# Fused attention and gated-MLP block on one core: where a kept tail of x stands, when the words of A11 are made, which queue stores the last round, and the order of the last sums

## The chip, the cores and the metric

The kernel runs on 1 core of one Trainium2 chip. The metric is device time in microseconds of one execution. The engines are TensorE (PE, its weight loads PEld), VectorE (DVE), ScalarE (ACT), GpSimd (POOL) and SyncE (SP); GpSimd and SyncE also issue the DMAs.

## The reference

```python
# x: 2048 x 576, wqkv: 576 x 1728, wo: 576 x 576, w_gate, w_up: 576 x 4608, w_down: 4608 x 576, all float32
xn = _layernorm(x, axis=-1)
s = _A_ref(xn, A_wqkv, A_wo)     # linear attention, 32 heads: phi(q) (phi(k)^T v) / (phi(q) . sum phi(k)), then @ wo
g = _silu(_B_ref(xn, B_w_gate, B_w_up, B_w_down))   # h = gelu(xn @ w_gate) * (xn @ w_up); h @ w_down
return x + s * g
```

## The kernel before

**Float32 from words.** A float32 operand is kept as two words: `hi`, a rounded copy that ScalarE writes, and `lo`, the rest, which VectorE subtracts (`cut_w`, `cut_two`, `cut`, `make_words`). A product is three matmuls: hi.hi, hi.lo, lo.hi.

**Three stages.** Up to about 210 us the attention's q, k and v are made, from 210 to 277 us the attention's output `s`; then come the gate and up projections (277 to 1073 us), then the down projection (to the end).

**Gate and up.** The two projections are 36 matrices, `q` = 0 to 35: even ones gate, odd ones up, 256 columns each. Rows and columns are halved, and each matrix is done with 7 block products instead of 8, on sums of blocks: weight blocks A11, S2, S1, S3, A12, S4, A22 against x blocks B11, T2, T1, T3, B21, B22, T4. x stands in two blocks of 1024 positions, s = 0 and s = 1, both halves of a product for both blocks at once. The products write into PSUM tiles named `al` (first and fifth), `be` (second), `ga` (third and sixth), `de` (fourth and seventh): the fifth to seventh accumulate onto what the first, third and fourth left there, so VectorE must have read it before.

288 input columns per half don't divide by 128: the last 32, the tail, are multiplied by themselves. The tail's words of x stand in plane 2 of one of the T tiles, and `TAIL` names which T tile of which block carries which of the two column halves. A tail's matmuls are the last of a product's early half and of its late half. The tail of the first column half (c = 0) is used by the fifth and the seventh product, that of the other by the third and the sixth.

Each product is worked in two halves, an early one and a late one. In step n the program issues the early half of product n, then what stands behind product n - 2 (`post_0` to `post_6`: reading PSUM, gelu or the multiplication with the up value, and the work of `todo`), then the late half of product n - 1. ScalarE and VectorE take their instructions in that order, so what is put in `todo[0]` stands in VectorE's queue in front of the sums of `post_1` and `post_2`. `todo` holds the preparation of the next matrix (`mat_pieces`: words of A11, of the sums S1 to S3, of A12 and A22, of S4), the sums of its blocks on GpSimd (`mat_sums`), the load of the one after it, and events.

Block 0 of x doesn't fit beside the attention's data. Its tiles are stored to HBM when they are made (`keep`, `form_apart`; 90 to 130 us) and loaded back (`back`) shortly before 277 us: B11, T2, T1 and T3 by GpSimd's queue, then B21, matrix 1, B22 and T4, in this order, by SyncE's. Their places in SBUF are those of attention data, which come free with the last matmul of `s`.

**h and its sums.** The 18 gate and up pairs form 9 macros (`m` = 0 to 8) of 4 matrices. The down projection also uses fewer products: 26 products `p` on sums of blocks of h. Those sums are added by GpSimd while the matrices run (`ADDS`, `add_up`), at hooks counted 7 to a matrix and 28 to a macro, and every value in `FORM` is stored to HBM (`put_out`). The sums of macro m run into the first matrices of macro m + 1. In the last macro, m = 8, the order is `ADDS_LAST`, the stores go by GpSimd's queue, and what is left behind the last matrix is added by VectorE.

**Down.** For each p and k tile, h is loaded in 5 units (`load_unit`), cut into words (`cut`, unit number u = 5p + k), and multiplied by words of w_down (`make_words`, in two parts: the first five k tiles and the last four). `down_first` gives the hooks of the last matrix the first loads, words and cuts; `down_all` does the rest, with `cut(u + 2)` ahead of the matmuls of unit u.

Of the kernel before, what the change touches and what calls it, by code (L numbers as in the profile page):

```python
# [8 lines left out]
F32 = mybir.dt.float32  # L9
# [47 lines left out]
NM = NG // 2  # L57
# [35 lines left out]

MAIN = ((0, 0), (0, 2), (2, 0), (1, 1), (1, 3), (3, 1))
XW = (0, 1, 3, 4)
TAIL = ({"T4": 0, "T1": 1}, {"T4": 0, "T3": 1})
TR = P // 2

X_SLOT = {"B11": 0, "B21": 1, "B22": 3, "T1": 9, "T3": 10, "T2": 11, "T4": 2}
# [3 lines left out]
def block_kernel(ctx, tc, x, xe, xt, wq_d, wkv_d, wo, wgu_d, wd_d, out):  # L103
    nc = tc.nc
# [52 lines left out]
    def dma(out, in_, eng=None):  # L157
        tc.keep_in_program_order((eng or nc.sync).dma_start(out=out, in_=in_))
# [21 lines left out]
    xo, xf, xstat, store = [{}, {}], [{}, {}], {}, {}  # L180
# [167 lines left out]
    def kept_words(nm, o):  # L348

        if nm in TAIL[0]:  # L350
            return o.rearrange("p k t -> p (k t)")
# [4 lines left out]
    def kept_place(nm, d):  # L356

        if nm in TAIL[0]:
            return d.rearrange("p k t -> p (k t)")
        return d.rearrange("p (a b) t -> p a (b t)", a=2)  # L360

    def kept(s, nm):
        store[s, nm] = d = dr.tile(
            [P, 5 if nm in TAIL[0] else 4, TBN], F32, name=f"kept_{s}_{nm}"
        )
        return d

    def keep(s, nm, o):
        if (s, nm) in store:
            for k in (0, 3):  # L370
                dma(out=store[s, nm][:, k : k + 2], in_=o[:, k : k + 2].bitcast(F32))
            return
        d = kept(s, nm)
        dma(out=kept_place(nm, d), in_=kept_words(nm, o.bitcast(F32)))

    def tail(s, b, o):

        h = s * TR
        for j in range(2):
            v = xf[s][BS[b][j]][:, 2, :]  # L380
            r, low = (slice(i + j * KR, i + (j + 1) * KR) for i in (h, TR - h))
            act(o[r], v[r], AF.Copy)
            vec("tensor_sub", o[low], v[r], o[r].bitcast(F32))
# [4 lines left out]
    def form_lo(s, nm, o):  # L388
        vec("tensor_sub", o[:, 3:5], xf[s][nm][:, 0:2], o[:, 0:2].bitcast(F32))
        if nm in TAIL[s] and nm != "T4":  # L390
            tail(s, TAIL[s][nm], o[:, 2, :])

# [189 lines left out]
    def run(todo, n=None):  # L582
        for _ in range(len(todo) if n is None else min(n, len(todo))):
            todo.pop(0)()
# [71 lines left out]
    at = {}  # L656
# [240 lines left out]
    raw, sums, wt = {}, {}, {}  # L897
# [34 lines left out]
    def quarters(q):  # L932
        return raw[q][:, 0:4].rearrange("p (j k) (f c) -> p j f k c", j=2, f=2)

    def cut_w(o, src):

        act(o[:, :, 0:2, :], src, AF.Copy)
        vec("tensor_sub", o[:, :, 2:4, :], src, o[:, :, 0:2, :].bitcast(F32))
# [14 lines left out]
    def mat_pieces(q):  # L953

        if q >= NQ:
            return [[] for _ in range(7)]

        def raws_(q=q):
            rv = quarters(q)
            if q % 2 == 0:  # L960
                cut_w(wt["b"][:, 1:3], rv[:, 1])
            else:
                cut_w(wt["b"][:, 1:2], rv[:, 1, 0:1])
                cut_w(wt["b"][:, 0:1], rv[:, 1, 1:2])
            cut_tail(q)

        return [
            [lambda: cut_w(wt["a"][:, 0:1], quarters(q)[:, 0, 0:1])],
            [], [],
            [lambda: cut_w(wt["a"][:, 1:4], sums["sm"][:, 0:3])],  # L970
            [raws_],
            [
                lambda: cut_w(wt["b"][:, 3:4], sums["sm"][:, 3:4]),
                lambda: cut_two(wt["last"], sums["last"]),
            ],
            [],
        ]
# [115 lines left out]
    HOOKS = 28  # L1093
# [30 lines left out]
            free[place_of[m, v]] = at  # L1124

    def put_out(m, v, at):
        eng = nc.gpsimd if m == NM - 1 else nc.sync
        dma(out=hs_d[m][:, FORM.index(v)], in_=value(m, v), eng=eng)
        used(m, v, at + 1)

# [80 lines left out]
    def load_reg(at, nm, third=None):  # L1211
        if at not in reg:
            b = big(REG[at], [P, ODD_W if REG[at] in ODD else REG_W], F32, f"b_{at}")
            reg[at] = b[:, 0 : KT * HALF].rearrange("p (k d) -> p k d", k=KT)
        j, c = int(nm[0]) - 1, int(nm[1]) - 1
        par, f = divmod(KP[j], 2)
        src = wd_d[par::2, :, f, c * HALF : (c + 1) * HALF].rearrange("g p d -> p g d")
        k = slice(0, KT) if third is None else slice(3 * third, 3 * third + 3)
        dma(out=reg[at][:, k], in_=src[:, k])
# [42 lines left out]
    def cut(u):  # L1262
        p, k = divmod(u, NU)
        if p >= NP:
            return
        hi, lo = hi_place(p, k), raw_v[p, k]
        hi_v[p, k] = hi
        src = lo.bitcast(F32)
        act(hi, src, AF.Copy)
        vec("tensor_sub", lo, src, hi.bitcast(F32))  # L1270
# [54 lines left out]
    def make_words(p, c):  # L1325

        if p >= NP or p in SHARED or (p, c) in made:
            return
        made.add((p, c))
        hi, lo = (w[c] for w in word_tiles(p))  # L1330
        src = reg[FROM[p]][:, HALVES[c]]
        if PROD[p][2]:
            act(hi, src, AF.Copy, scale=-1.0)
            vec(
                "scalar_tensor_tensor", lo, src, -1.0, hi.bitcast(F32),
                op0=ALU.mult, op1=ALU.subtract,
            )
        else:
            act(hi, src, AF.Copy)
            vec("tensor_sub", lo, src, hi.bitcast(F32))  # L1340
# [101 lines left out]
    def down_first():  # L1442

        return [
            [lambda: load_reg("22", "22")],
            [lambda: load_reg("42", "42")],
            [],
            [lambda: load_unit(0, 0), lambda: load_unit(0, 1), lambda: make_words(0, 0)],
            [
                lambda: load_unit(0, 2), lambda: load_unit(0, 3), lambda: load_unit(0, 4),  # L1450
                lambda: make_words(0, 1), lambda: cut(0),
            ],
            [lambda: load_reg("32", "32"), lambda: cut(1)],
            [],
        ]

# [5 lines left out]
    def down_all():  # L1462
        late = []
        last = NP - 1
        for u in range(NP * NU):
            p, k = divmod(u, NU)
            n = KT * p + 2 * k
            for at in sorted(events):
                if at <= H_END + n // 2:
                    run_events(at)  # L1470
            if p in LOADS and k < 3:
                load_reg(*LOADS[p], k)
            if k == 0:
                for o, e in ENDS.items():
                    if e == p:
                        load_sx(o)
            if k < 2:
                change(p + 1, k)
                if p in SHARED:
                    make_words(p + 1, k)  # L1480
            elif k < 4:
                make_words(p + 1, k - 2)
                if p + 1 in SHARED and p:
                    make_words(p + 2, k - 2)
            if p == last and k == 0:
                read(p - 1)
                late += closings(p - 1)
            if p == last and k == 1:
                run(late, 1)
            cut(u + 2)  # L1490
            if p == last and k == 2:
                break
            for kt in range(*UNITS[k]):
                down_mm(p, kt, range(TT))
            load_unit(p + 1, k)
            run(stores)
            if p == last:
                continue
            if k == 1 and p:
                read(p - 1)  # L1500
                late += closings(p - 1)
            else:
                run(late, 2)
        run(late)
        run(stores)
        o = next(o for o, e in ENDS.items() if e == last)
        for j in (TT - 2, TT - 1):
            add_in(o, j, last)
        for j in range(TT):
            for kt in range(UNITS[2][0], KT):  # L1510
                down_mm(last, kt, (j,))
            late += close_last(o, j, last, j >= TT - 2)
            run(late, len(late) - 1)
        run(late)
# [166 lines left out]
    def form_apart(nm):  # L1681

        f = xf[0][nm]
        d = kept(0, nm)
        hi, lo, last = (slot([P, 2, TBN], F32R, f"xo_0_{nm}_{i}") for i in range(3))
        act(hi, f[:, 0:2], AF.Copy)
        vec("tensor_sub", lo, f[:, 0:2], hi.bitcast(F32))
        tail(0, TAIL[0]["T4"], last[:, 0])
        dma(out=d[:, 0:2], in_=hi.bitcast(F32))
        dma(out=d[:, 2:4], in_=lo.bitcast(F32))  # L1690
        dma(out=kept(0, "T4")[:, 2], in_=last[:, 0].bitcast(F32))

    behind = {
        (0, 0): [
# [54 lines left out]
    def first_matrix():  # L1749
        w_tile("a", 15)  # L1750
        return mat_pieces(0)
# [17 lines left out]
        (0, 1): [lambda: scale(1, 0, 1), lambda: halve(1, 0, 1)],  # L1769
        (0, 2): [lambda: scale(1, 2, 3, 4), lambda: halve(1, 2, 3, 4)],  # L1770
        (0, 3): [lambda: back("T1"), lambda: mat_sums(0)],
        (1, 0): [lambda: pieces.extend(first_matrix()), lambda: run(pieces[0])],
        (1, 1): [lambda: run(pieces[3])],
    }
    pieces = []
    for tb in (2, 3, 0, 1):
# [85 lines left out]
```

## Time and profile before

| | |
|---|---|
| runs | 1452.13, 1450.04, 1450.32 us; median 1450.32 |
| profiled execution | 1454.09 us, span 1452.4 us, mean granted TensorE clock 0.996 |
| TensorE busy | 1435.6 us (99%) |
| VectorE, ScalarE, GpSimd busy | 1006.7, 578.2, 542.7 us |
| DMA | 228.16 MB, 157 GB/s over the span |

In timelines a row is: start, duration, engine, line, operation, output<-inputs with buffer numbers left out, and in brackets the idle time before it with what ended it. xo is block 1 of x, xr the reloaded block 0; `_B` and `_T` are the B and T blocks. wa and wb hold weight words; wa the A11 and the sums S1 to S3, wb the others. spot_h, spot_m and spot_g are places of h and its sums, hs their store in HBM; raw is the loaded weight matrix, raw_a, raw_b and raw_h loaded units of h, bd the down projection's PSUM. Matmul rows are half-width tiles in pairs, one for each block. eps_t rows are marks by which ScalarE follows TensorE.

### The profile page before, as it was taken

How to read it: one execution, taken by the hardware profiler on the slowest of the kernel's cores; microseconds unless marked ns; L12 is line 12 of the kernel's file. 1: busy time of each engine (PE TensorE's matmuls, PEld its weight loads, DVE VectorE, ACT ScalarE, POOL GpSimd, SP SyncE). 2: the span in 40 equal slices, each digit the busy share in tenths (PEclk: the TensorE clock that was granted, in tenths of full speed). 3: DMA queues.
4: the chain of work that ended last, by engine and by line, in shares of the span. 5: the costliest groups of instructions: out<-in, count | busy, mean ns of one | idle time of the engine just before them, and what ended most of it. 6: DMA issues, size and time to landing. Idle time of an engine off the chain costs nothing.

```text
span 1452.4 us, 29230 instructions
## 1 busy us (share of the span) xinstructions
PE 1435.6 (99%) x11656; PEld 1361.9 (94%) x11656; DVE 1006.7 (69%) x1519; ACT 578.2 (40%) x1249; POOL 542.7 (37%) x556
## 2 busy tenths in 40 slices
PE   9999999989999999999999999999999999999998
PEld 8989989889999999999999999999889999999998
DVE  7788666245666656657555666656768978989897
ACT  6354365333222333322333222333236555545454
POOL 3342340115755557475465755557532000000000
PEclk9999999999999999999999999999999999999999
DMA  5444115512332314233232322314279888767886
GB/s 213 172 192 155 45 36 189 215 46 74 132 113 103 132 55 160 95 120 114 78 141 74 136 109 102 132 55 160 77 268 359 259 263 254 244 191 233 280 290 218
DMA packets 120579, 228.16 MB, mean 157 GB/s; under 512 B 11674, under 2 KB 45370, under 8 KB 119802
## 3 DMA queue, kind: packets, MB, share of 16 engines
q1 hardware_dynamic: 117258, 214.82, 43.6%
q0 software_dynamic: 3040, 11.27, 2.1%
q8 instruction: 92, 1.51, 0.4%
q14 instruction: 45, 0.37, 0.1%
q10 hardware_dynamic: 144, 0.20, 0.0%
HBM read 144.93 MB, written 81.27 MB: 156 GB/s over the span
## 4 chain that ended last, share of the span: by engine, by line
PE 89%; DVE 5%; DMA 2%; issue 1%; ACT 1%; SPq 0%; POOL 0%; ACTq 0%; DVEq 0%; POOLq 0%
PE bd L152 21%; PE ga L152 17%; PE de L152 15%; PE al L152 15%; PE kv L152 7%; PE be L152 6%; PE s L152 4%; PE q L152 2%; DMA raw_h<-hs 1%; DMA xr_T<-kept_T 1%; PE kv_a L152 1%; DVE raw_h L149 1%; DVE xo_T L149 1%; DVE wa L149 0%; DVE sx L149 0%
## 5 line engine op out<-in xcount | busy, mean ns | idle before, releaser
L155 POOL TENSOR_TENSOR sums<-raw 128x256 f32<-128x256 f32 (+1 forms) x108 | 70.4, 652 | 165.0 <-DMA raw<-in_wgu_dram 124.0
L152 PE MATMUL de<-xr_T,wa 64*128 64x512 f32 x486 | 128.8, 389 | 0.0
L152 PE MATMUL de<-xo_T,wa 64*128 64x512 f32 x486 | 128.6, 389 | 0.0
L152 PE MATMUL kv<-wkv,xo_B 128*128 128x412 f32 (+2 forms) x662 | 125.0, 347 | 0.1
L152 PEld LDWEIGHTS kv<-wkv,xo_B 128*128 128x128 f32 x662 | 120.2, 188 | 1.5 <-ACT xo_B L146 0.6
L152 PE MATMUL de<-xo_T,wb 64*128 64x512 f32 x486 | 121.6, 386 | 0.0
L152 PE MATMUL ga<-xo_T,wa 64*128 64x512 f32 x486 | 121.6, 386 | 0.0
L152 PE MATMUL de<-xr_T,wb 64*128 64x512 f32 x486 | 121.6, 386 | 0.0
L152 PE MATMUL ga<-xr_T,wa 64*128 64x512 f32 x486 | 121.6, 386 | 0.0
L149 DVE TENSOR_TENSOR wa<-raw,wa 128x256 fp32r<-128x256 f32 x54 | 48.4, 897 | 102.0 <-ACT wa L146 102.0
L152 PE MATMUL bd<-w_head,hi 128*128 128x288 f32 x516 | 117.7, 294 | 0.0
L152 PE MATMUL ga<-xo_B,wb 64*128 64x512 f32 x432 | 112.2, 393 | 2.2 <-DVE spot_m L149 2.2
L152 PE MATMUL ga<-xr_B,wb 64*128 64x512 f32 x432 | 112.0, 393 | 0.0
L152 PE MATMUL al<-xr_B,wb 64*128 64x512 f32 x432 | 109.9, 387 | 0.0
L152 PE MATMUL al<-xr_B,wa 64*128 64x512 f32 x432 | 109.5, 386 | 0.0
L152 PE MATMUL al<-xo_B,wa 64*128 64x512 f32 x432 | 109.5, 386 | 0.0
L152 PE MATMUL al<-xo_B,wb 64*128 64x512 f32 x432 | 109.5, 386 | 0.0
L152 PE MATMUL be<-xo_T,wa 64*128 64x512 f32 x432 | 109.4, 386 | 0.0
L152 PE MATMUL be<-xr_T,wa 64*128 64x512 f32 x432 | 109.4, 386 | 0.0
L146 ACT ACTIVATE hi<-raw_h 128x1024 fp32r<-128x1024 f32 x59 | 62.4, 1059 | 86.1 <-PE bd L152 58.0
L152 PEld LDWEIGHTS de<-xo_T,wa 64*128 64x128 f32 x486 | 90.3, 186 | 4.0
L152 PEld LDWEIGHTS de<-xr_T,wa 64*128 64x128 f32 x486 | 90.1, 186 | 3.1
(300 smaller groups left out, 4754.4 us busy)
## 6 DMA issues: line engine op xcount, KB each, us to landing
raw_h<-hs SPq DMA_DIRECT2D x176, 256.0 KB
raw<-in_wgu_dram SPq DMA_DIRECT2D x36, 640.0 KB
hs<-spot_h SPq DMA_DIRECT2D x90, 256.0 KB
hs<-spot_g SPq DMA_DIRECT2D x80, 256.0 KB
b<-in_wd_dram SPq DMA_DIRECT2D x42, 432.0 KB
hs<-spot_m SPq DMA_DIRECT2D x38, 256.0 KB
raw_g<-hs SPq DMA_DIRECT2D x22, 256.0 KB
raw_a<-hs SPq DMA_DIRECT2D x20, 256.0 KB
```

The costliest lines, as they stand in the source:

```text
L146: pin(nc.scalar.activation(*args, **kw))
L149: pin(getattr(nc.vector, op)(*args, **kw))
L152: pin(nc.tensor.matmul(*args, **kw))
L155: pin(getattr(nc.gpsimd, op)(*args, **kw))
```

## The change

Four edits:

- The tail of c = 0 of block 0 is kept in plane 2 of T3 instead of T4. T3 is then stored and loaded with 5 planes of 256 KB and T4 with 4; T4 is stored by one DMA instead of two. The fifth and seventh products read block 0's tail from T3. Block 1 is as before.
- The words of A11 for the next matrix are made in `todo[3]`, behind the words of S1 to S3, instead of `todo[0]`. For matrix 0 the order stays.
- In the last macro stores at hooks before 21 of it (the first three matrices) are issued by SyncE; those from the last matrix on stay with GpSimd.
- In the hooks of the last matrix `cut(0)` and `cut(1)` stand in hook 4, `cut(2)` and then the second part of the first words in hook 5; before, it was those words and `cut(0)` in hook 4, `cut(1)` in hook 5, and `cut(2)` at the start of the down projection, behind the sums of the sixth and seventh products.

```diff
-TAIL = ({"T4": 0, "T1": 1}, {"T4": 0, "T3": 1})
+TAIL = ({"T3": 0, "T1": 1}, {"T4": 0, "T3": 1})
...
     def keep(s, nm, o):
-        if (s, nm) in store:
-            for k in (0, 3):
-                dma(out=store[s, nm][:, k : k + 2], in_=o[:, k : k + 2].bitcast(F32))
-            return
         d = kept(s, nm)
...
         return [
-            [lambda: cut_w(wt["a"][:, 0:1], quarters(q)[:, 0, 0:1])],
-            [], [],
-            [lambda: cut_w(wt["a"][:, 1:4], sums["sm"][:, 0:3])],
+            [], [], [],
+            [
+                lambda: cut_w(wt["a"][:, 1:4], sums["sm"][:, 0:3]),
+                lambda: cut_w(wt["a"][:, 0:1], quarters(q)[:, 0, 0:1]),
+            ],
...
     def put_out(m, v, at):
-        eng = nc.gpsimd if m == NM - 1 else nc.sync
+        eng = nc.gpsimd if at >= HOOKS * m + 21 and m == NM - 1 else nc.sync
...
             [
                 lambda: load_unit(0, 2), lambda: load_unit(0, 3), lambda: load_unit(0, 4),
-                lambda: make_words(0, 1), lambda: cut(0),
+                lambda: cut(0), lambda: cut(1),
             ],
-            [lambda: load_reg("32", "32"), lambda: cut(1)],
+            [lambda: load_reg("32", "32"), lambda: cut(2), lambda: make_words(0, 1)],
...
-            cut(u + 2)
+            if u:
+                cut(u + 2)
...
         act(hi, f[:, 0:2], AF.Copy)
         vec("tensor_sub", lo, f[:, 0:2], hi.bitcast(F32))
-        tail(0, TAIL[0]["T4"], last[:, 0])
+        tail(0, TAIL[0][nm], last[:, 0])
         dma(out=d[:, 0:2], in_=hi.bitcast(F32))
-        dma(out=d[:, 2:4], in_=lo.bitcast(F32))
-        dma(out=kept(0, "T4")[:, 2], in_=last[:, 0].bitcast(F32))
+        dma(out=d[:, 3:5], in_=lo.bitcast(F32))
+        dma(out=d[:, 2], in_=last[:, 0].bitcast(F32))
...
-        (1, 0): [lambda: pieces.extend(first_matrix()), lambda: run(pieces[0])],
-        (1, 1): [lambda: run(pieces[3])],
+        (1, 0): [lambda: pieces.extend(first_matrix()), lambda: run(pieces[3][1:])],
+        (1, 1): [lambda: run(pieces[3][:1])],
```

## The prediction

> **What bounds the kernel.** I read the page first, then the waits of TensorE, the windows around the longest of them, and the timelines of the engines named there. The page:
>
> ```profile
> span 1452.4 us, 29230 instructions
> PE 1435.6 (99%) x11656; PEld 1361.9 (94%) x11656; DVE 1006.7 (69%) x1519; ACT 578.2 (40%) x1249; POOL 542.7 (37%) x556
> ```
>
> TensorE is busy for all but 1452.4 - 1435.6 = 16.8 us, and the change removes no matmul. It can gain only in those gaps and where matmuls run at a lower clock. TensorE's waits (total, times, longest) name the gaps, and three windows (columns: length, busy time of PE, PEld, DVE, ACT, POOL, then granted clock, DMA share, GB/s) give the clock behind them:
>
> ```profile
> PE al L152 <- DMA xr_T<-kept_T: 5.3, 1, 5.3
> PE ga L152 <- DVE spot_m L149: 2.2, 1, 2.2
> ...
> PE bd L152 <- DVE raw_b L149: 1.1, 1, 1.1
> ...
> PE bd L152 <- DVE raw_a L149: 0.4, 1, 0.4
> ...
> 294.30:301.00 6.70, 6.66 (x34) 5.26 (x36) 1.29 (x2) 0.38 (x3) 0.00 (x0) 0.53 0.00 0
> ...
> 1038.00:1060.00 22.00, 19.79 (x158) 15.70 (x156) 10.81 (x19) 8.15 (x21) 6.42 (x7) 0.92 0.26 88
> ...
> 1080.00:1088.00 8.00, 6.91 (x52) 6.68 (x51) 5.65 (x5) 1.06 (x1) 7.05 (x9) 1.00 1.04 394
> ```
>
> Behind the 5.3 us wait the clock is 0.53 for 6.7 us, behind the 2.2 us wait it is low too (0.92 over 22 us), behind the 1.1 us wait it stays 1.00. So the first two cost more than their length. What each costs in all is read by comparing with the same stretch of an undisturbed pass (601 to 607 us): first matrix, pass at 600, last round.
>
> ```profile
> 288.70 0.39 PE L152 MATMUL al<-xo_T,wa 64*128 64x512 f32 x1
> 294.35 0.79 PE L152 MATMUL al<-xr_T,wa 64*128 64x512 f32 x1 [5.25 <-DMA xr_T<-kept_T]
> ...
> 302.15 0.39 PE L152 MATMUL de<-xo_T,wb 64*128 64x512 f32 x1
> ...
> 601.81 0.39 PE L152 MATMUL al<-xo_T,wa 64*128 64x512 f32 x1
> ...
> 603.37 0.39 PE L152 MATMUL de<-xo_T,wa 64*128 64x512 f32 x1
> 603.40 0.39 PE L152 MATMUL ga<-xo_B,wb 64*128 64x512 f32 x1
> ...
> 606.80 0.39 PE L152 MATMUL de<-xo_T,wb 64*128 64x512 f32 x1
> ...
> 1038.57 0.39 PE L152 MATMUL de<-xo_T,wa 64*128 64x512 f32 x1
> 1041.16 0.74 PE L152 MATMUL ga<-xo_B,wb 64*128 64x512 f32 x1 [2.21 <-DVE spot_m L149]
> ...
> 1046.42 0.39 PE L152 MATMUL de<-xo_T,wb 64*128 64x512 f32 x1
> ```
>
> From the tail of the fifth product (al<-xo_T,wa) to the seventh product (de, wb) the undisturbed pass takes 606.80 - 601.81 = 4.99 us, the first matrix 302.15 - 288.70 = 13.45: 8.46 us lost, 5.25 in the wait and the rest at the low clock. From the last de, wa to de, wb it takes 606.80 - 603.37 = 3.43, in the last round 1046.42 - 1038.57 = 7.85: 4.42 us lost.
>
> **Part 1: the tail kept with T3.** The fifth product no longer reads block 0's T4 (the last of four loads on SyncE: B21, matrix 1, B22, T4) but T3, which the fourth product reads anyway. T4 is next asked for by the seventh. The tail adds 256 KB to T3's load on GpSimd's queue and takes them off T4's. The stores of T3 and T4 around 94 to 130 us move the same bytes, with one DMA fewer, under TensorE work without a wait there: nothing. What is late next:
>
> ```profile
> 276.55 0.74 POOL L158 DMA_DIRECT2D xr_T<-kept_T  x1 [10.06 <-PE s L152]
> ...
> xr_T<-kept_T POOLq DMA_DIRECT2D x2, 1024.0 KB, 6.2
> ...
> xr_T<-kept_T POOLq DMA_DIRECT2D x1, 1280.0 KB, 8.0
> ...
> 284.14 0.39 PE L152 MATMUL de<-xo_T,wa 64*128 64x512 f32 x1
> ...
> 287.44 0.47 PE L152 MATMUL al<-xr_B,wb 64*128 64x512 f32 x1
> ...
> 288.93 0.42 ACT L146 ACTIVATE wa<-raw 128x256 fp32r<-128x256 f32 x1 [4.73 <-DMA raw<-in_wgu_dram]
> ...
> 291.11 1.27 DVE L149 TENSOR_TENSOR spot_h<-u,ga 128x512 f32<-128x512 f32 x2
> ```
>
> T3 is issued at 276.55. With 1280 KB it takes between 6.2 (as 1024 KB did) and 8.0 us (as T1's 1280 KB did): it lands between 282.75 and 284.55, asked for at 284.14, so it costs 0 to 0.4 us. Matrix 1 lands at 288.93, T4 at 294.3; between them lie B22's 1024 and T4's 1280 KB, so 427 KB/us (an estimate from these two rows), and B22 lands near 291.3, or 0.6 us later if T3's extra 256 KB push the queue behind it. The sixth product (ga, wb) needs B22 and is due at 288.70 + (603.40 - 601.81) = 290.3. I take it to start at 291.9, the later end, because T3 goes ahead on the same engines; in that is a wait of up to 0.6 us for B21, whose first use at 287.44 has no slack that the trace shows. The seventh product follows 606.80 - 603.40 = 3.40 us later, at 295.3; T4 is there at 294.3. It started at 302.15: **gain 6.8 us**. Best end: B22 in time and T4 at 294.3 sets the start, 7.8 us. Worst end: the new waits, about 1.6 us, also drop the clock for one stretch as the 2.2 us wait did (4.42 - 2.59 + 0.03 = 1.86 us), and T3 is late: 4.5 us. The 1.1 us wait, which left the clock at 1.00, is the nearer row.
>
> That the sixth product can start at 291.9 rests on part 2: it accumulates onto ga, which VectorE read at 291.11 to 292.38 in the first matrix. That was late only because A11's words stood ahead of it, waiting for the matrix of 288.93.
>
> **Part 2: A11's words behind the fourth product, and the last round's stores.** In VectorE's queue the cut of A11 stood in front of the sums of al, be and ga. The fast case, the long one, and POOL beside it:
>
> ```profile
> 597.85 1.37 DVE L149 TENSOR_TENSOR wa<-raw,wa 128x256 fp32r<-128x256 f32 x1 [1.99 <-ACT wa L146]
> ...
> 619.61 0.43 DVE L149 TENSOR_TENSOR wa<-raw,wa 128x256 fp32r<-128x256 f32 x1 [4.17 <-ACT wa L146]
> ...
> 1033.05 6.26 DVE L149 TENSOR_TENSOR wa<-raw,wa 128x256 fp32r<-128x256 f32 x1 [1.99 <-ACT wa L146]
> ...
> 1037.14 0.56 POOL L158 DMA_DIRECT2D hs<-spot_h  x1
> ...
> 1055.92 3.32 SPq L158 DMA_DIRECT2D b<-in_wd_dram  x2
> ```
>
> The same instruction takes 0.43 us alone, 1.37 beside GpSimd's adds, and 6.26 in the last round, where GpSimd also issues stores. The sums behind it free ga, on which TensorE waits until 1041.16. Either edit alone ends this: moved, the cut has nobody behind it that the sixth product needs; with the stores of that stretch on SyncE, it would cost 1.37 as in all other rounds, which show no wait. On SyncE each store waits for the sum that it carries; queued behind them are only the weight loads that are issued at 1055.92, after the last of those sums, so nothing is held up: 0. **Gain 4.4 us**, both ends (4.0 to 4.4).
>
> The Trainium skill (SBUF — State Buffer, section "SBUF: two separate sides") says that VectorE with two SBUF inputs and GpSimd lock a shared port for a whole instruction. The 1.37 us row agrees; 6.26 us is more than one add. By that rule alone the long row would be 1.4 us and this term 0 (a sum of 7.3), by the trace the term is 4.4; since the long row is there, the rule gets no chance of its own. The skill (TensorE: Matmul & The Clock Gate, "What's actually happening") lets the clock fall after an idle window of about 3.4 us; here 2.2 us sufficed.
>
> **What the move costs in the other passes.** A11's cut now comes behind that of the three sums. In half of the passes GpSimd adds there:
>
> ```profile
> 628.44 1.90 POOL L155 TENSOR_TENSOR spot_h<-spot_g,spot_h 128x512 f32<-128x512 f32 x1
> ...
> 629.10 1.27 DVE L149 TENSOR_TENSOR spot_h<-spot_h,al 128x512 f32<-128x512 f32 x2
> ...
> 631.96 0.39 PE L152 MATMUL al<-xo_B,wa 64*128 64x512 f32 x1
> ...
> 650.93 0.96 DVE L149 TENSOR_TENSOR wa<-sums,wa 128x768 fp32r<-128x768 f32 x1 [2.34 <-ACT wa L146]
> ...
> 651.12 1.93 POOL L155 TENSOR_TENSOR spot_g<-spot_g,spot_h 128x512 f32<-128x512 f32 x1
> ...
> 653.72 0.39 PE L152 MATMUL al<-xo_B,wa 64*128 64x512 f32 x1
> ```
>
> In an up pass with adds the cut waits for the add that ends at 628.44 + 1.90 = 630.34 and takes some 0.4; the two products with al behind it (1.27) end at 632.0 instead of 630.4, and TensorE wants al's banks at 631.96: 0 to 0.1 us. In a gate pass with adds the add ends at 653.05, the cut at 653.4, TensorE wants the words at 653.72. Both fit, barely; one add more (1.3) wouldn't. Sixteen passes are of these kinds: I take **0.5 us in all**, ends 0 and 4 (0.5 us in each of eight).
>
> **Part 3: the first words of h ahead of the last sums.** No work is added; VectorE's order changes. Before, cuts 0, 1 and 2 stood between the second half of the first words and the sums of the sixth and seventh products; now cuts 0 and 1 stand first, and cut 2 and those words ahead of the last sums.
>
> ```profile
> 1080.37 1.95 DVE L149 TENSOR_TENSOR raw_b<-raw_b,beside 128x1024 fp32r<-128x1024 f32 x1
> 1082.25 1.21 DVE L149 TENSOR_TENSOR raw_b<-raw_b,hi 128x1024 fp32r<-128x1024 f32 x1
> ...
> 1085.38 0.29 PE L152 MATMUL bd<-w_end,hi 128*128 128x288 f32 x1
> ```
>
> The listed waits for raw_b (cut 2, 1.1) and raw_a (cut 1, 0.4) go. Cut 3 stays behind the same sum of work and still ends near 1082.25 + 1.21 = 1083.5; TensorE, which asked for it at 1085.38, would ask near 1083.9 or, with the smaller gaps also gone, 1083.3. So cut 3 is late next, by 0 to 1 us. **Gain 1.0 us**, ends -0.5 and 2.0.
>
> **Sum.** 6.8 + 4.4 - 0.5 + 1.0 = 11.7 us. The profiled execution took 1454.09 us (1.7 around its span), 3.8 above the median 1450.32; so 1442.4 on its scale, 1438.6 on that of the runs.
>
> **Rivals.** (B) The A11 cut misses by half a microsecond in the eight gate passes with adds: the margin of 0.3 us speaks for it, the hi words, which are ready earlier, against it. 3.5 us less gain: 1442.1. (C) Block 0's loads hold TensorE longer and the clock falls in the first matrix: gain there 4.5 or less, 1441 to 1443. For it: four loads land within 10 us; against it: the 1.1 us wait. (D) The new order of cuts only hands the wait on to cut 3: 1439.6 to 1440.1. (E) The other side: the A11 cut loses one more add of 1.3 us in all sixteen passes, so that both the al banks and the words are late by over 1 us each time: some 18 us, 1457. It decides from (11.7 + 0.5) / 16 = 0.76 us a pass on. The margins speak for it; against it, the rows above repeat the same order in every round, with one add per cut.
>
> **How the numbers follow.** The forecast 0.52 (its own range 1435.5 to 1441), B 0.16, C 0.14, D 0.14, E 0.04. The range runs from all best ends (7.8 + 4.4 + 2.0 - 0 = 14.2, 1436.1, a little lower for the scatter of the runs) to C and B, 1444. 0.2% is 2.9 us, about what this measurement can tell from no change: faster holds for all but E and for B and C together at their worst: 0.92, same 0.05, slower 0.03.
>
> **What would show it.** Right: no wait of al for xr_T; a wait of about 1 us for xr_B near 291; granted clock 1.00 in both stretches; wa<-raw never over 2 us; no store on GpSimd's queue before the last matrix; raw_b's wait gone. Wrong: al waiting for wa or for its own banks every fourth pass; a low clock near 292; waits for cut 3 over 1 us.

## The result, and the profile after

The changed kernel took 1441.2 us (median of 4 runs, 1439.22 to 1443.47) beside 1450.47 us (median of 4, 1450.04 to 1452.13): ratio 0.9934 (0.9917 to 0.9952), 9.3 us faster. In two later batches it took 1440.46 and 1441.39 (5 runs each); all its 14 runs have a median of 1440.6, some 9.9 below the kernel before, whose batches have medians of 1450.42 to 1450.85. Forecast were 1438.6 us and a gain of 11.7. So 1441.2 lies 0.2 us above the range that the prediction gave its main case (1435.5 to 1441), and within that of all its cases (1436.1 to 1444).

The profiled execution took 1439.22 us (span 1437.5), the fastest of the 14. That of before, at 1454.09, was among its kernel's slowest. So the two traces differ by 14.9 us in span and the medians by 9.3 to 9.9; which part of the 14.9 counts needed more traces. First the page of the changed kernel, then TensorE's waits (total, times, longest), then three windows (columns as in the prediction, the granted clock behind POOL's time):

```profile
span 1437.5 us, 29286 instructions
...
PE 1429.8 (99%) x11656; PEld 1386.1 (96%) x11656; DVE 1009.7 (70%) x1519; ACT 578.8 (40%) x1249; POOL 539.3 (38%) x550
```

```profile
PE idle L152 <- POOL ident masks.py:199: 1.6, 1, 1.6
PE ga L152 <- DVE spot_h L149: 0.8, 1, 0.8
PE bd L152 <- DVE raw_b L149: 0.2, 1, 0.2
```

```profile
290.80:297.50 6.70, 6.67 (x58) 6.68 (x60) 1.87 (x3) 4.70 (x10) 0.93 (x2) 1.00 0.08 34
1034.00:1056.00 22.00, 22.00 (x197) 21.42 (x195) 10.75 (x20) 8.91 (x23) 1.45 (x2) 1.00 0.46 150
1070.00:1078.00 8.00, 7.77 (x59) 7.53 (x58) 5.89 (x5) 3.45 (x4) 6.95 (x8) 1.00 1.05 412
```

The waits for xr_T (5.3) and spot_m (2.2) are gone, and the clock is 1.00 in both places where it was 0.53 and 0.92. TensorE's rows, in the first matrix and in the last round:

```profile
283.50 0.39 PE L152 MATMUL de<-xo_T,wa 64*128 64x512 f32 x1
...
288.10 0.39 PE L152 MATMUL al<-xo_T,wa 64*128 64x512 f32 x1
...
289.69 0.39 PE L152 MATMUL ga<-xo_B,wb 64*128 64x512 f32 x1
290.82 0.46 PE L152 MATMUL ga<-xr_B,wb 64*128 64x512 f32 x1 [0.75 <-DVE spot_h L149]
...
294.18 0.39 PE L152 MATMUL de<-xo_T,wb 64*128 64x512 f32 x1
...
1030.58 0.39 PE L152 MATMUL de<-xo_T,wa 64*128 64x512 f32 x1
...
1030.62 0.39 PE L152 MATMUL ga<-xo_B,wb 64*128 64x512 f32 x1
...
1034.02 0.39 PE L152 MATMUL de<-xo_T,wb 64*128 64x512 f32 x1
```

From al<-xo_T,wa to de, wb the first matrix now takes 294.18 - 288.10 = 6.08 us (13.45 before, 4.99 undisturbed). In the last round the stretch from the last de, wa to de, wb takes 1034.02 - 1030.58 = 3.44 (7.85 before, 3.43 undisturbed). And VectorE's queue:

```profile
286.89 1.29 DVE L149 TENSOR_TENSOR spot_h<-u,ga 128x512 f32<-128x512 f32 x2 [1.83 <-PE ga L152]
290.09 1.29 DVE L149 TENSOR_TENSOR spot_h<-spot_h,de 128x512 f32<-128x512 f32 x2 [1.92 <-PE de L152]
296.18 0.96 DVE L149 TENSOR_TENSOR wa<-sums,wa 128x768 fp32r<-128x768 f32 x1 [4.80 <-ACT wa L146]
297.06 0.42 DVE L149 TENSOR_TENSOR wa<-raw,wa 128x256 fp32r<-128x256 f32 x1
```

VectorE read ga at 286.89, 4.2 us earlier than before (291.11), with the A11 cut now at 297.06. The row at 290.82 names VectorE's spot_h as what ended the wait, yet that sum had ended at 288.18: by the DMAs' completions in the trace, it was B22, which landed at 290.69.

**One table for all traces.** Every kernel here issues the same 11,656 matmuls, so a stretch of the program is the time between the starts of the same two numbered matmuls (us): first matrix (numbers 1900 to 2200), steady passes (2200 to 8500), last round (8500 to 8700), start of the down projection (8840 to 9100). The last column is the time from the issue of the load of raw_a for the second down product (the first of four) to the start of ScalarE's hi words of it.

```
                     first matrix  steady  last round  down start  raw_a load
before                   43.39     714.00    27.10       36.68       10.74
before_b                 42.79     714.00    25.78       36.60       10.40
e1_tail                  37.01     714.00    27.39       37.80       11.41
e2_words                 42.59     714.00    22.67       37.76       12.14
e3_stores                41.63     714.00    22.67       36.47       10.33
e4_cuts  (new order)     42.86     714.00    25.76       35.03       10.23
after    (new order)     36.02     714.00    22.67       34.97       10.20
after_b  (new order)     36.03     714.00    22.67       38.12       11.55
e8_both  (new order)     36.06     714.00    22.67       39.53       12.56
e5_order (new order)     34.97     714.00    22.67       35.09       10.28
e5_b     (new order)     35.00     714.00    22.67       40.78       11.83
e6_nocuts                35.83     714.00    22.67       36.49       10.75
e9_both                  35.28     714.00    22.67       36.45       10.15
```

before_b is the kernel before again, after_b and e8_both the changed one. e1_tail to e4_cuts have one edit each, e6_nocuts all but the new order of the first cuts ("new order" marks the kernels that have it). e5_order and e5_b are the changed kernel with B22 loaded ahead of matrix 1, e9_both is that without the new order. All are told below. A last run, e7_sync, issues that load some 17 us later and is left out for it; its first four columns are 35.01, 714.00, 22.67 and 48.73.

### The profile page after: what moved, and what is told of

Its sections match the earlier page's. It is cut to its first block, busy times and chain, and to the rows that moved or that the text cites. A ratio compares the mean times of both kernels' runs of the same rounds, so it can differ in the third digit from the quotient of the medians.

```text
span 1437.5 us, 29286 instructions
## 1 busy us (share of the span) xinstructions
PE 1429.8 (99%) x11656; PEld 1386.1 (96%) x11656; DVE 1009.7 (70%) x1519; ACT 578.8 (40%) x1249; POOL 539.3 (38%) x550
## 4 chain that ended last, share of the span: by engine, by line
PE 93%; DVE 4%; DMA 1%; ACT 1%; issue 1%; SPq 0%; POOL 0%; ACTq 0%; DVEq 0%; POOLq 0%
PE bd L152 22%; PE ga L152 17%; PE al L152 15%; PE de L152 15%; PE kv L152 8%; PE be L152 7%; PE s L152 4%; PE q L152 2%; DMA raw_h<-hs 1%; PE kv_a L152 1%; DVE xo_T L149 1%; DVE raw_h L149 0%; PE idle L152 0%; DVE w_end L149 0%; PE d L152 0%
## 5 line engine op out<-in xcount | busy, mean ns | idle before, releaser
L149 DVE TENSOR_TENSOR u<-u,be 128x512 f32<-128x512 f32 x72 | 46.3, 685 | 84.7 <-PE be L152 72.4
L152 PEld LDWEIGHTS ga<-xo_T,wa 64*128 64x128 f32 x486 | 89.4, 184 | 1.6
```

Source lines behind the costliest of these rows:

```text
L149: pin(getattr(nc.vector, op)(*args, **kw))
L152: pin(nc.tensor.matmul(*args, **kw))
```

## The experiments

**One edit each, added to the kernel before** (all beside the same runs of it, median 1450.47). The tail alone:

```diff
-TAIL = ({"T4": 0, "T1": 1}, {"T4": 0, "T3": 1})
+TAIL = ({"T3": 0, "T1": 1}, {"T4": 0, "T3": 1})
...
```

> Kernel before with the tail kept with T3 alone. My theory: the wait of al for T4 goes, but A11's words still stand ahead of the sums in VectorE's queue and wait for matrix 1 (288.9), so ga is read only at about 292.4 and the sixth product starts there instead of at 290.3: a wait of 2 us for VectorE, behind which the clock falls for one stretch of 3.4 us as it did behind the 2.2 us wait. Gain 4.5 us against the 7.3 us that the whole change shows in that place; 6.3 if the clock holds. Rival: the tail alone brings the whole 7 us, and the move of A11's words has no part in it.

1446.26 us, ratio 0.9970 (0.9960 to 0.9979), so 4.2 us gained. With the A11 cut still in front, VectorE reads ga late and TensorE waits, but only for 0.7 us:

```profile
288.79 0.62 DVE L149 TENSOR_TENSOR wa<-raw,wa 128x256 fp32r<-128x256 f32 x1 [9.58 <-ACT wa L146]
...
290.52 1.27 DVE L149 TENSOR_TENSOR spot_h<-u,ga 128x512 f32<-128x512 f32 x2
```

```profile
291.25 0.50 PE L152 MATMUL ga<-xo_B,wb 64*128 64x512 f32 x1 [0.71 <-DVE spot_h L149]
```

The tail alone brings 42.65 - 37.01 = 5.6 us of the first matrix (42.65 is the mean of the five traces without it). The moved A11 cut is worth another 1.0 there (37.01 to 36.03): what the theory left it in case the clock holds (7.3 - 6.3), not the 2.8 of its main case. No clock falls there.

A11's words alone:

```diff
-            [lambda: cut_w(wt["a"][:, 0:1], quarters(q)[:, 0, 0:1])],
-            [], [],
+            [], [], [],
...
+                lambda: cut_w(wt["a"][:, 0:1], quarters(q)[:, 0, 0:1]),
...
```

> Kernel before with A11's words behind the fourth product alone; the last round's stores stay on GpSimd's queue. My theory: the 2.2 us wait for VectorE in the last round and the low clock behind it go, 4.4 us, and the wait for T4 in the first matrix stays at about 5.3 us: span about 1448. In the passes with adds nothing is lost. Rival: the words come too late in sixteen passes, up to 0.5 us each, so that less than 2 us are left.

1448.34 us, ratio 0.9987 (0.9978 to 0.9995): 2.1 us gained where 4.4 were expected. The last round falls to 22.67; the steady passes keep 714.00, so the move costs nothing in them.

The last round's stores alone:

```diff
-        eng = nc.gpsimd if m == NM - 1 else nc.sync
+        eng = nc.gpsimd if at >= HOOKS * m + 21 and m == NM - 1 else nc.sync
```

> Kernel before with the last macro's early stores on SyncE alone; A11's words stay where they were. My theory: the long row of A11's cut (6.3 us) comes from GpSimd's issuing of stores beside its adds, so it shrinks to the 1.4 us of the other rounds, the wait of ga in the last round goes and 4.4 us are gained, as many as by the move of the words alone. Rival: the long row comes from the adds alone; then it stays over 5 us and nothing is gained.

1447.15 us, ratio 0.9975 (0.9966 to 0.9984): 3.3 us gained where 4.4 were expected. The last round falls to the same 22.67, this time with the A11 cut still in front of the sums. VectorE's cut, which took 6.26 in before, and GpSimd's adds beside it:

```profile
1030.87 1.36 DVE L149 TENSOR_TENSOR wa<-raw,wa 128x256 fp32r<-128x256 f32 x1 [1.99 <-ACT wa L146]
```

```profile
1029.41 1.29 POOL L155 TENSOR_TENSOR spot_h<-spot_h,spot_h 128x512 f32<-128x512 f32 x1
1030.65 1.29 POOL L155 TENSOR_TENSOR spot_g<-spot_g,spot_h 128x512 f32<-128x512 f32 x1
1031.91 1.48 POOL L155 TENSOR_TENSOR spot_h<-spot_h,spot_h 128x512 f32<-128x512 f32 x1
```

The cut gets in after one add. In before it got in after five:

```profile
1032.16 1.30 POOL L155 TENSOR_TENSOR spot_h<-spot_h,spot_h 128x512 f32<-128x512 f32 x1
1033.42 1.28 POOL L155 TENSOR_TENSOR spot_g<-spot_g,spot_h 128x512 f32<-128x512 f32 x1
1034.67 1.28 POOL L155 TENSOR_TENSOR spot_h<-spot_h,spot_h 128x512 f32<-128x512 f32 x1
1035.91 1.28 POOL L155 TENSOR_TENSOR spot_g<-spot_g,spot_h 128x512 f32<-128x512 f32 x1
...
1037.72 1.29 POOL L155 TENSOR_TENSOR spot_h<-spot_h,spot_g 128x512 f32<-128x512 f32 x1
```

It began at 1033.05 and ended at 1039.31, 0.3 us after the fifth add (1037.72 + 1.29 = 1039.01). So taking the stores off GpSimd ends the long cut: shown. (The cut takes 6.26 us in all four traces that have both the old place of the cut and these stores: before, before_b, e1_tail and e4_cuts.) That the store instructions themselves are what holds it is not shown: without them the adds also start 0.6 us earlier against the cut, and in before the first four adds ran back to back, with no store between them until 1037.14, and the cut still waited. The Trainium skill (SBUF — State Buffer, section "SBUF: two separate sides") lets the engine that starts first keep the shared port for a whole instruction; one add and the cut, 1.36, agrees with that, while five adds in front of a waiting cut are more than the sentence says.

The order of the first cuts alone:

```diff
-                lambda: make_words(0, 1), lambda: cut(0),
+                lambda: cut(0), lambda: cut(1),
...
-            [lambda: load_reg("32", "32"), lambda: cut(1)],
+            [lambda: load_reg("32", "32"), lambda: cut(2), lambda: make_words(0, 1)],
...
```

> Kernel before with the new order of the first cuts of h alone. My theory: the waits for raw_a and raw_b at the start of the down projection go, and a wait of 0.2 us for cut 3 comes: 2 us gained there, nothing elsewhere. Rival: cut 3 takes over the wait and nothing is gained.

1450.46 us, ratio 1.0001 (0.9992 to 1.0010): no gain in the median, though the interval leaves room for 1.2 us, and its profile shows the start of the down projection at 35.03 instead of 36.6.

**The changed kernel and three relatives.** In the run without the new order, the cuts stand as before and all other edits stay. In the run with another order of loads, B22 goes ahead of matrix 1 on SyncE's queue (all four go by SyncE in every kernel; where an expectation says "all on SyncE's queue", it means this order):

```diff
-    back("B21", eng=nc.sync)
+    back("B21", "B22", eng=nc.sync)
     load_mat(1)
-    back("B22", "T4", eng=nc.sync)
+    back("T4", eng=nc.sync)
```

> Changed kernel with SyncE's loads in the order B21, B22, matrix 1, T4 instead of B21, matrix 1, B22, T4. My theory: in the changed kernel the sixth product of the first matrix waits 0.75 us for B22, though the profile names VectorE, which had read ga 2.6 us before. With B22 ahead of matrix 1 that wait goes and the first matrix is 0.7 us shorter; matrix 1 lands 2.4 us later, its sums are then still in time for the words. Rival: the wait is VectorE's or moves to T4, and the first matrix stays as long.

> The changed kernel once more, for a second profile and more runs. If the 14.9 us between the two profiles overstated the change, by low-clock stretches that fell into the profile of before and not into that of the changed kernel, then the median stays near 1441 (9 to 10 us gained) and this profile has a span near 1439 to 1441 with at least one stretch at half clock or a slower stretch elsewhere. Rival: 1437.5 is its usual span, and the median falls below 1440.

> Changed kernel with the old order of the first cuts of h, so the other three edits alone. The new order alone gave no gain in the median, though its profile shows the start of the down projection 1.5 to 2.7 us shorter. If the new order is worth 2 us, this kernel is 2 us slower than the changed one; if it is worth nothing, both have the same median, and the time comes back somewhere behind the start of the down projection.

> The kernel before once more, for a second profile. If its first profile (span 1452.4) was long because three stretches at half clock fell into it, this one has a span near 1449 with one or two of them; the passes between the first matrix and the last round take 714.0 us again, and the start of the down projection 36.5 to 37.8 us.

1440.12, 1440.46, 1440.42 and 1450.85 us (5, 5, 5 and 11 runs; before 1450.42). With B22 ahead of matrix 1 the sixth product no longer waits:

```profile
289.91 0.39 PE L152 MATMUL ga<-xo_B,wb 64*128 64x512 f32 x1
...
290.13 0.39 PE L152 MATMUL ga<-xr_B,wb 64*128 64x512 f32 x1
```

The first matrix goes from 36.03 to 34.97. As VectorE's order is untouched, this shows that the 0.8 us wait, and some 0.3 behind it, were B22's load.

Without the new order the median is that of the changed kernel, 1440.42 beside 1440.46. The second trace of the changed kernel shows what can take the gain back. One of TensorE's waits, and the cut that it names:

```profile
PE bd L152 <- DVE raw_a L149: 2.8, 1, 2.8
```

```profile
1076.23 3.52 DVE L149 TENSOR_TENSOR raw_a<-raw_a,hi 128x1024 fp32r<-128x1024 f32 x1 [2.61 <-ACT hi L146]
```

```profile
1076.13 1.29 POOL L155 TENSOR_TENSOR spot_h<-spot_g,spot_h 128x512 f32<-128x512 f32 x1
1077.38 1.27 POOL L155 TENSOR_TENSOR spot_g<-spot_h,spot_g 128x512 f32<-128x512 f32 x1
```

This is the first cut of the second down product (u = 5). In the first trace it was

```profile
1074.44 1.44 DVE L149 TENSOR_TENSOR raw_a<-raw_a,hi 128x1024 fp32r<-128x1024 f32 x1 [1.29 <-ACT hi L146]
...
1076.35 0.29 PE L152 MATMUL bd<-w_head,raw_a 128*128 128x288 f32 x1
```

and ended at 1075.88, 0.5 us before TensorE's first matmul on those words. In the second trace two things came together. The load took 11.55 us instead of 10.20, so the cut began 1.35 us later against its issue, and it then stood behind two adds of GpSimd and took 3.52 us instead of 1.44. Less the 0.5 us to spare, that makes 3.0 us, for a wait of 2.8.

**Whether the stores from the last matrix on matter too, and how the changed kernel scatters.** In e7_sync (the other order of loads) no store goes by GpSimd:

```diff
-        eng = nc.gpsimd if at >= HOOKS * m + 21 and m == NM - 1 else nc.sync
+        eng = nc.sync
```

> The changed kernel with the four late loads all on SyncE's queue as in the run before, and now every store of the last macro issued by SyncE, none by GpSimd. Theory: a cut on VectorE is held over several instructions of GpSimd where GpSimd issues a store between two adds (6.26 us in the last round before the change, 3.52 us for raw_a at the start of the down projection in one of two profiles of the changed kernel). With no store on GpSimd no cut between 1060 and 1085 us takes over 2.0 us, no wait for raw_a or raw_b exceeds 0.5 us, and the time is that of the run with SyncE's loads alone less 0.3 to 1.0 us, so about 1439.4. Rival: the order on SyncE's queue decides: the stores wait there for GpSimd's sums, the loads of raw_a and raw_b queued behind them are issued later, a wait on a DMA of raw_a or raw_b over 1 us appears at the start of the down projection, and the time is 1441 to 1444. Second rival: the 3.52 us are adds back to back and have nothing to do with stores: cuts of 2.5 us or more remain, and the time stays at 1440.1.

> The changed kernel with B21, matrix 1, B22 and T4 all loaded by SyncE, once more, to see which waits come back from one execution to the next. Theory: the first matrix stays at 35.0 us (its wait is gone for good, since it hung on a queue), while the wait for raw_a at the start of the down projection comes and goes by up to 2.8 us with the moment at which the loads land; median 1439.5 to 1440.7. Rival: the first matrix varies too, 35 to 36.1.

> The changed kernel as it is, once more beside the other two, for a comparison on one chip. First matrix 36.0 us with a wait of 0.7 to 0.9 us for ga, last round 22.67 us, start of the down projection either 35.0 (no wait over 0.5 us) or 38 (a wait of 2 to 3 us for raw_a); median 1440 to 1441.2, so 0.3 to 1 us above the run with SyncE's loads.

1451.31, 1440.10 and 1441.39 us (before 1450.52). The first is as slow as the kernel before (ratio 1.0006, 0.9997 to 1.0015), and its first rival is what happened, at a higher price than the 1441 to 1444 us that it named. SyncE's queue:

```profile
1065.84 2.92 SPq L158 DMA_DIRECT2D hs<-spot_h  x3
1069.77 0.32 SPq L158 DMA_DIRECT2D hs<-spot_g  x1
1070.18 1.28 SPq L158 DMA_DIRECT2D hs<-spot_h  x2
1076.32 3.71 SPq L158 DMA_DIRECT2D hs<-spot_g  x2
1080.12 1.83 SPq L158 DMA_DIRECT2D raw_a<-hs  x4
```

```profile
PE bd L152 <- ACT hi L146: 9.7, 1, 9.7
```

The stores wait for GpSimd's sums, and the loads behind them are issued at 1080.12 (1063.14 in after). TensorE waits 9.7 us, and behind that the clock is low (0.51 from 1086 to 1092 us): the start of the down projection takes 48.73 us (35.0 in e5_order). The change leaves just these stores with GpSimd. The adds ran at other times here, so this run says nothing on what holds the cuts.

The repeats show the changed kernel at 34.97, 38.12 and 39.53 us at the start of the down projection (35 or 38 were expected for the third, and a median of up to 1441.2), and the variant with the other loads at 35.09 and 40.78. In the last one TensorE ran at half clock behind a 2.7 us wait for raw_a (window as above):

```profile
1078.00:1084.00 6.00, 5.84 (x24) 5.84 (x25) 5.96 (x6) 2.54 (x4) 1.79 (x3) 0.50 0.51 173
```

**The other order of loads with the old order of cuts:**

> The changed kernel with the four late loads on SyncE's queue and the old order of the first cuts. Theory: the new order gained nothing in the median, because the waits that it removes (0.4 and 1.1 us) had kept TensorE behind the next cut, that of raw_a for the second product: with the old order the start of the down projection takes 36.4 to 37.9 us in every execution, with the new one 35.0 where the load of raw_a lands within 10.3 us of its issue and 38 to 41 where it takes 11.5 or more. So here: first matrix 35.0 us, last round 22.67, start of the down projection 36.4 to 37.9 with waits for raw_a of 0.4 and raw_b of 1.0, and a median of 1439.2 to 1440.0, at or a little under the 1440.1 of the new order with the same loads. Rival: the late load decides in either order: waits of 2 us or more for raw_a here too, a start of 38 us or more in the profile, the median at 1440.5 or above.

1441.10 us (1440.38 to 1441.95). The start of the down projection is 36.45 with waits of 0.4 and 1.0, as the theory said; the median is not, it lies where the rival put it. The profiled execution was the fastest of the five, and what the others lost no trace shows. Of the two orders: the ten runs with the old one and all else changed lie between 1440.2 and 1442.2, the 24 with the new one between 1438.0 and 1444.4. That the new order widens the scatter agrees with the table; whether it gains or loses in the median these runs can't tell.

Lowest of all is the changed kernel with B22 ahead of matrix 1: 1440.1 us in ten runs, ratios 0.9929 (0.9916 to 0.9941) and 0.9933 (0.9920 to 0.9945). Its trace is 1.05 us better in the first matrix; against the changed kernel's 1440.6 the runs can't show as little.

## Why the prediction was right, and where it was off

**Part 1, right.** T3 was issued at 275.94 and landed at 282.3 by the DMAs' completions, before the fourth product at 283.50 asked for it, so near the lower end. The wait for B22 came (0.75 listed, 1.1 over the undisturbed pass: 6.08 - 4.99) and no clock fell. On its profile 7.4 us are gained (13.45 - 6.08) for a forecast of 6.8. The difference is the 0.6 us by which the prediction let B22 come later: this trace stands 0.6 us earlier than that of before (288.10 for 288.70), so B22's 290.69 is 291.3 on the scale of before, where it had landed at 291.28, and the seventh product's 294.18 is 294.8 there, for a forecast of 295.3. Over all traces the gain is 42.65 to 36.04, 6.6. That it rests in part on the A11 cut was right in kind; that part is 1.0 us.

**Part 2, right in mechanism, too sure of its size.** "Either edit alone ends this" was shown by two runs, both at 22.67 us. "Gain 4.4 us, both ends (4.0 to 4.4)" failed in the lower end: 1.3 us of it was the low clock behind the 2.2 us wait, and that doesn't happen every time. The same wait in the second trace of before, and the clock over the same 22 us:

```profile
PE ga L152 <- DVE spot_m L149: 2.2, 1, 2.2
```

```profile
1035.00:1057.00 22.00, 19.69 (x170) 17.43 (x168) 12.16 (x18) 8.32 (x22) 8.37 (x9) 1.00 0.22 76
```

The clock stayed at 1.00 and the round took 25.78 instead of 27.10. So the gain is 3.1 in two of the four traces with that wait and 4.4 and 4.7 in the other two, 3.8 in the mean. The prediction read the term in one execution, one with the low clock, and subtracted it from the median of the runs. The rule of the Trainium skill that it cited (TensorE: Matmul & The Clock Gate, "What's actually happening": the clock falls after an idle window of about 3.4 us) doesn't separate the cases: the waits of 2.2 to 2.8 us are all shorter than its window, and some were followed by a low clock and some not.

**What the move costs, taken at 0.5 us: 0.00.** The steady passes take 714.00 us in every trace, and the longest A11 cut is now 1.52 us (duration ns: min/median/max):

```profile
L149 DVE TENSOR_TENSOR wa<-raw,wa x54: 418/421/1520, 266.4 to 1035.5; 128x256 fp32r<-128x256 f32 x54
```

Rivals B and E are out. So is C, though 1441.2 lies in its range of times: the clock held in the first matrix (1.00).

**Part 3, right for cut 3 and wrong in what comes behind it: 1.0 us forecast, no gain clear of the scatter.** "Cut 3 is late next, by 0 to 1 us" was right (the wait for raw_b is 0.2). The step that failed is that it stopped there. Before, the waits of 0.4 and 1.1 us for cuts 1 and 2 held TensorE back by 1.5 us, and the cut of the second product's first unit had that much more time. Where its load was early (10.2 to 10.8 us from issue to use), that cut ended 1.5 to 2.2 us ahead of TensorE's first matmul on its words in the old order and 0.5 us ahead in the new one. But the load takes between 10.2 and 12.6 us, and the cut, 1.2 us at its shortest, takes up to 3.5 where it meets GpSimd's adds.

The table's last two columns in the new order: 10.20, 10.23 and 10.28 give 34.97, 35.03 and 35.09; 11.55, 11.83 and 12.56 give 38.12, 40.78 and 39.53, with waits of 2.5 to 2.8 us, cuts of 3.52, 3.23 and 2.50, and in the last two a low clock (0.50) on top. In the old order 10.15 to 10.75 give 36.45 to 36.68. A load of 11.41 with a cut of 3.24 (e1_tail) made TensorE wait 0.8 us and gives 37.80. One of 12.14 with a short cut (e2_words) made no wait at all; the 37.76 there come from another wait, for raw_b some 10 us later:

```profile
1083.02 1.23 DVE L149 TENSOR_TENSOR raw_a<-raw_a,hi 128x1024 fp32r<-128x1024 f32 x1 [3.75 <-ACT hi L146]
...
1095.03 0.40 PE L152 MATMUL bd<-w_end,raw_b 128*128 128x288 f32 x1 [0.90 <-DVE raw_b L149]
```

So the new order gains 1.5 us where the load is early; where it is late, its three traces are 0.3 to 3 us longer than the two of the old order. That is rival D, with another cut at the end of it. What delays the load by 2 us from one execution to the next stays open; the DMA share there is 1.05, so the engines that move it are full.

**The sum.** 6.6 + 3.8 + 0 - 0.4 (start of the down projection, mean of six traces in the new order against seven in the old: 37.25 - 36.89) = 10.0 us, for 9.9 measured over all runs and 11.7 forecast. The last term is rough: the six lie between 34.97 and 40.78, which makes their mean good to about 1 us. Against the forecast 0.2, 0.6 and 1.4 us are missing in the three parts, and the 0.5 us kept for the move was not needed. Single edits bring 4.2 (tail), 2.1 or 3.3 (words or stores, one stall) and 0.0; the tail and the stores give 7.5, with the 1.0 of the words in the first matrix 8.5; the 1.4 left to 9.9 is within the intervals of the two (about 1.4 and 1.3 to each side). Why the words alone bring less than the stores alone isn't settled; the intervals overlap. Both bring less than the 4.4 expected of them, which was read from a trace with the low clock; the mean over the traces is 3.8.

## What to carry to other kernels

Before a wait is booked as a gain, look for the next thing that it was shielding: follow the engine's next two or three demands and compare each margin with how much that transfer's landing varies. Read a stall's price in more than one execution, or split it into the wait itself and what the clock adds. When stores leave one queue for another, list what is queued behind them there: for stores ahead of the weight loads it cost nothing, for those ahead of h's loads 9.7 us of waiting.

## What had not been expected of the hardware

- A VectorE subtraction beside GpSimd's adds of 1.3 us can stand behind one add, two or five: 1.36 and 6.26 us for a cut that takes 0.42 alone, 3.52 us for a larger one that takes 1.22. What lets it in is open: in the case of two no store was issued between them, and in the case of five none between the first four.
- The same gap of TensorE has different prices: 2.2 us was followed by a low clock in the traces of before and e1_tail (last round 27.10 and 27.39) and not in before_b and e4_cuts (25.78 and 25.76); a 2.7 us wait was followed by a clock of 0.50 in e5_b, one of 2.8 us in after_b by no such stretch.
